# Two-bank score tiles, one exponential for two heads, a third column group as quads, and an earlier start of LayerNorm rows

## The chip, the cores and the metric

The kernel runs on one core of a Trainium2 chip. The metric is the device time of one execution in microseconds (us); less is better. TensorE (PE) does the matrix products, VectorE (DVE), ScalarE (ACT) and GpSimd (POOL) the rest, and SyncE (SP) issues most of the transfers.

## The reference

A transformer layer in fp32, with LayerNorm ahead of both halves, for 2048 tokens of width 640, 32 heads of 20, an inner width of 1536 and a causal window of 256.

```python
q, k, v = split(layernorm(x) @ wqkv)                 # 32 heads of 20
scores = q @ k.T * 20 ** -0.5                        # masked to 0 <= i - j < 256
h = x + (softmax(scores) @ v) @ wo
n = layernorm(h)
out = h + (gelu(n @ w_gate) * (n @ w_up)) @ w_down   # gelu by tanh
```

## The kernel before, in words

**Numbers.** Each fp32 factor is split into two f16 parts, a high and a low one (`xh`, `xl`, `w5h`, `w5l` and so on), and a product is the sum of three: high by high, high by low, low by high. All instructions go through one helper, so every row of the profile names line 199; they are told apart by the names of their tiles.

**Attention.** The 2048 tokens are 16 blocks of 128 queries, each with a window of up to three blocks of keys. The 32 heads are 16 pairs, the even head in the upper and the odd head in the lower half of PE's rows. Each row of work is done twice: `maxima` computes q by k into PSUM and `max_out` takes the greatest of each query on DVE (tile `junk`, with the result in `mxs`); `scores` computes k by q with the maxima subtracted through extra rows of `qT` and `kT`, and `score_out` takes the exponential on ACT into `pt`. POOL masks `pt`, and PE multiplies it by `v` into `pv`. Then come the product by `wo`, the row `h` (tile `ht`, stored by SP to `h_dram` for the end), and its LayerNorm.

**PSUM.** `bank(name)` hands out banks of rings: `mm` (2 banks), `ra` and `rb` (2 each), `pv` and `tp` (1 each). A row of maxima or scores takes both banks of `ra` or `rb`, one for each head; `two(name)` says when both are free. `row_need` chooses what the next row is. `ra` and `rb` also serve the early LayerNorm transposes and the scales of weights.

**Feed-forward.** Four chunks `c` of 512 tokens by three groups `fg` of 512 inner columns, in the order of the list `ORDER`: (0,0), (1,0), (0,1), (0,2), (1,1), (1,2), then chunks 2 and 3. The first `PLAIN` of these are done by `gate_up`: for each of four `ft` steps 30 matmuls of 512 columns into `mm`. The others are done by `quad`, which gets the same sums from nine spans of five matmuls (10 of 512 and 35 of 256 columns) into `tp`, `ra`, `pv` and `rb`, with the help of sums of weights (`weight_sums`, tile `ws`, made by POOL and DVE) and of tokens (`token_sums`, tile `ts`, made by DVE). Weight sums are stored to `wsums` and later loaded rather than made again, as `QLOAD` lists. `down` multiplies by `w_down` and adds into `ht`; between quads it fills PE. The names in the trace: `w5`/`w8` are gate and up of group 1, `w6`/`w9` of group 2, `gu` of group 0; `w10`, `w11`, `w12` are `w_down`; `h0h`/`h0l` and `h1h`/`h1l` are the normalised chunks.

**LayerNorm of h.** `first_norm_lane` normalises the four blocks of chunk 0 during the attention, from their tiles `ht` (`B[b].h`) into a tile `lxn`. `norm_start` starts two lanes of `norm_lane` for each later chunk: load a block's row from `h_dram` into a `wsl` tile, statistics (`lsth`, `lsti`), power by POOL, normalise, split, and turn it by DMA into the chunk's tiles, which for chunk 2 are those of chunk 0.

**Order.** No order is written out by hand. The kernel runs through lanes (generators) and a model of each engine's time (`Clock`); at each step it issues what the model says can start first. So a changed duration or a changed condition anywhere can change the order of everything after it. On the chip each engine runs its instructions in that recorded order. While no score has been issued and PE would stand idle in the model, a small matmul `pv<-ident16` is issued as filler.

Of the kernel before, what the change touches and what calls it, by code (L numbers as in the profile page):

```python
# [11 lines left out]
F32 = mybir.dt.float32  # L12
# [10 lines left out]
P = 128  # L23
# [230 lines left out]
def block_kernel(ctx: ExitStack, tc: tile.TileContext, x, wqkv, wo, wg, wu, wd, out):  # L254
# [9 lines left out]

    banks = dict(mm=2, ra=2, rb=2, pv=1, tp=1)

    opened, pos = Counter(), Counter()

    def bank(name, dt=F32):
        opened[name] += 1  # L270
        return nc.tile(psum, [P, 512 if dt == F32 else 1024], dt, name, banks[name])

# [29 lines left out]
    def need(*reads, slots=(), when=None, eng="tensor"):  # L302

        def f():
            if when and not when() or any(opened[n] >= banks[n] for n in slots):
                return INF
            return max([nc.ready(reads, eng)]
                       + [nc.slot(psum, n, banks[n]) for n in slots])
        return f
# [222 lines left out]
    def products(n, term, ready=None, at_=None):  # L532


        ps = [at_[0]] if at_ else []
        col = at_[1] if at_ else 0

        def start(i):
            if ready and not ready(i) or not ps and opened["mm"] >= banks["mm"]:
                return INF  # L540
            t = nc.ready([x for ab in term(i) for x in ab], "tensor")
            return t if ps else max(t, nc.slot(psum, "mm", banks["mm"]))

        for i in range(n):
            yield ("tensor",), lambda i=i: start(i)
            if not ps:
                ps.append(bank("mm"))
            m = term(i)
            for k, (l, r) in enumerate(m):
                if k:  # L550
                    yield pe()
                o = ps[0][:, col:col + r.free_size()]
                nc.tensor.matmul(o, l, r, start=(i == 0 and k == 0),
                                 stop=(i == n - 1 and k == len(m) - 1))
                pos["dense"] += r.free_size() * 3 // len(m)
        return o
# [17 lines left out]

    attn = ExitStack()
    wqp = ExitStack()
# [237 lines left out]
    def maxima(at_):  # L814
        j, pr = heapq.heappop(maxq)
        b = B[j]
        ps = [bank(at_) for _ in range(2)]
        n = len(window(j))
# [12 lines left out]
    def two(name):  # L831

        if opened[name]:
            return INF
        return max(nc.slot(psum, name, banks[name], k) for k in range(2))

# [89 lines left out]
    def scores(at_):  # L926
# [3 lines left out]
        if pr % 2 == 0:  # L930
            b.pt[u] = at("pt", [P, 4, 3, P], F32, 3)
            pos["units"] += 1
        n = len(window(j))
        ps = [bank(at_)[:, :pairs(j) * n * P].rearrange("p (k a b) -> p k a b", a=n, b=P)
              for _ in range(2)]
        for k in range(pairs(j)):
            for i, kb in enumerate(window(j)):
                for par in range(2):
                    rs = slice(64 * par, 64 * par + 62)
                    nc.tensor.matmul(ps[par][:, k, i, :], kT[rs, pr + k, kb % RK, :],  # L940
                                     b.c.qT[rs, pr + k, b.cols], start=True, stop=True)
        for par in range(2):
            tasks.append(score_out(j, pr, par, ps[par], b.pt[u], at_))
        pos["score"] += pairs(j)

    def score_out(j, pr, par, ps, pt, at_):
        b = B[j]
        u = pr // 2
        n = len(window(j))
        m = pairs(j)  # L950
        yield on("scalar", ps)
        if m > 1:
            nc.scalar.activation(pt[:, par::2, :n, :], ps, AF.Exp, scale=esc)
        else:
            nc.scalar.activation(pt[:, 2 * (pr % 2) + par, :n, :], ps[:, 0], AF.Exp, scale=esc)
        done(at_)
        pos[j, u] += m
        if pos[j, u] < 4:
# [103 lines left out]
    ORDER += [(c, fg) for c in range(2, NCH) for fg in range(FG)]  # L1062
    PLAIN = 4
    hts, ga = {}, {}
# [201 lines left out]
    def norm_start(c):  # L1266
        yield ("sync",), need(when=lambda: pos["gu", c - 2] == FG if c > 1 else (
            ffpools[0] and W["d", 0].ready and all(b.wrote for b in B[CB:2 * CB])), eng="sync")
# [8 lines left out]
    def norm_lane(c, bs, lane, t):  # L1277
        for b in bs:
            j = c * CB + b
            yield ("sync",), lambda: nc.others(t, "sync")  # L1280
            nc.sync.dma_start(t, h_dram[j * P:(j + 1) * P, :])
            yield from layernorm(t, lane, *hpart(c, b), xn=lambda: t, dma=True)
            chunk[c] += 1
# [5 lines left out]
    def token_sums(c):  # L1289
        hh, hl = hT[c]  # L1290
        h1, h2 = hh[:, :, :CW], hh[:, :, CW:]
        l1, l2 = hl[:, :, :CW], hl[:, :, CW:]
        yield on("vector", when=lambda: ffpools[1] and (c == 1 or W["d", FG - 1].ready))
        t = (nc.tile(ffp, [P, KC, 512], F32, "ts") if c % 2 else
             nc.tile(ffpools[0], [P, KC, 512], F32, "wst")).bitcast(F16)
# [14 lines left out]
    WS = {}  # L1310
    QLOAD = [(c, fg) for c in range(2, NCH) for fg in range(FG) if (c, fg) != (2, 0)]
    wsums = dram.tile([FG * FT, P, 4 * KC * P], F16, name="wsums")
# [92 lines left out]
    def dense_lane():  # L1405
# [238 lines left out]
```

## Time and profile before

| | |
|---|---|
| Time, median of 3 runs | 1042.01 us (1041.12 to 1042.12) |
| The profiled execution's own time | 1043.35 us |
| Its span | 1041.6 us |
| Granted TensorE clock, mean | 0.996 |
| PE, DVE, ACT, POOL busy | 98%, 75%, 47%, 26% |

The attention takes about the first 600 us of the span, the feed-forward the rest, with its first groups mixed into the last of the attention. In a row of instructions the first two numbers are start and duration in us, or start of a run of `xN` instructions; in brackets stand the idle time of the engine before it and what ended it. Matmuls are pipelined, so their cost is read from start to start. In a row of a group the numbers behind the bar are busy time in us and the mean duration of one in ns, behind the second bar the idle time before them and what ended it. In a row of windows each engine has its busy time and instruction count, then come the granted clock, the share of DMA and GB/s.

### The profile page before, as it was taken

The page shows a single profiled execution, that of the slowest core. Times are in us where ns is not written, and L with a number is a line of the kernel's source. Part 1 is how long each engine was busy: PE and PEld are TensorE (multiplying, and loading weights), DVE is VectorE, ACT ScalarE, POOL GpSimd, SP SyncE. Part 2 cuts the span into 40 slices and gives each one's busy share as a digit, 9 for nine tenths or more (in the row PEclk, how much of TensorE's full clock was granted, in tenths as well). Part 3 has the DMA queues.
Part 4 walks back from the last instruction along what each step waited for, and adds up shares of the span by engine and source line. Part 5 has one row for each costly group of instructions (what it writes and reads, how often), then busy time and mean ns, then how long its engine had stood idle before and what let it go on. Part 6 is the DMA issues. An engine that isn't in the chain of part 4 may idle for free.

```text
span 1041.6 us, 26895 instructions
## 1 busy us (share of the span) xinstructions
PE 1019.7 (98%) x10802; PEld 691.2 (66%) x10802; DVE 778.4 (75%) x2193; ACT 490.6 (47%) x938; POOL 269.8 (26%) x369
## 2 busy tenths in 40 slices
PE   8999999999999999999999899999999999999998
PEld 7876567667666666676655564555777777777776
DVE  6878989998787777677687867676997985445553
ACT  6512667666666766666667835341122222222220
POOL 7100332233333323232323511031445310000000
PEclk9999999999999999999999999999999999999999
DMA  8663354361341513415302341314342652122211
GB/s 300 149 133 114 119 121 132 122 150 55 73 107 43 101 45 77 77 44 112 129 28 90 78 139 52 101 51 127 102 144 110 164 166 77 59 94 102 77 51 51
DMA packets 89116, 105.86 MB, mean 102 GB/s; under 512 B 22176, under 2 KB 63392, under 8 KB 88992
## 3 DMA queue, kind: packets, MB, share of 16 engines
q1 hardware_dynamic: 76896, 93.41, 31.2%
q10 hardware_dynamic: 12096, 10.75, 3.2%
q8 instruction: 84, 1.38, 0.6%
q14 instruction: 40, 0.33, 0.1%
HBM read 71.11 MB, written 28.84 MB: 96 GB/s over the span
## 4 chain that ended last, share of the span: by engine, by line
PE 78%; DVE 13%; issue 3%; DMA 3%; ACT 2%; POOL 0%; SPq 0%; DVEq 0%; ACTq 0%
PE mm L199 40%; PE pv L199 11%; PE ra L199 11%; PE rb L199 9%; PE tp L199 7%; DVE junk L199 4%; DMA qT<-qk 1%; DVE am L199 1%; DMA wst<-in_wd_dram 1%; DVE m L199 1%; DVE al L199 0%; DVE ht L199 0%; ACT pt L199 0%; DVE qks L199 0%; DMA wsl<-h_dram 0%
## 5 line engine op out<-in xcount | busy, mean ns | idle before, releaser
L199 POOL TENSOR_SCALAR_AFFINE_SELECT pt<-pt 128x512 f32<-128x512 f32 x240 | 152.9, 659 | 361.4 <-ACT pt L199 358.7
L199 DVE CUSTOM_DVE_ANT_0 junk<-rb,mask 128x384 bf16<-128x384 f32 (+2 forms) x262 | 138.9, 530 | 42.4 <-PE rb L199 22.6
L199 DVE CUSTOM_DVE_ANT_0 junk<-ra,mask 128x384 bf16<-128x384 f32 (+2 forms) x250 | 132.2, 529 | 41.4 <-PE ra L199 22.3
L199 ACT ACTIVATE pt<-ra,esc 128x384 f32<-128x384 f32 (+2 forms) x248 | 130.7, 579 | 68.4 <-PE ra L199 57.3
L199 ACT ACTIVATE pt<-rb,esc 128x384 f32<-128x384 f32 (+2 forms) x232 | 122.0, 578 | 70.1 <-PE rb L199 59.2
L199 PE MATMUL pv<-pt,v 128*21 128x128 f32 x2880 | 104.8, 277 | 2.1 <-ACT oT L199 2.1
L199 PEld LDWEIGHTS <-ah 128*128 128x128 f16 x768 | 75.5, 98 | 31.1 <-issue 3.1
L199 ACT ACTIVATE gel<-gel,ffk 128x512 f32<-128x512 f32 x32 | 23.1, 722 | 121.4 <-DVE gel L199 121.4
L199 PEld LDWEIGHTS pv<-pt,v 128*21 128x21 f32 x2880 | 68.8, 101 | 17.0 <-ACT oT L199 2.8
L199 PEld LDWEIGHTS <-kT 62*128 62x128 f16 x1440 | 57.8, 95 | 22.7 <-issue 12.7
L199 PEld LDWEIGHTS <-ws 128*128 128x128 f16 x640 | 62.6, 98 | 7.2
L199 PEld LDWEIGHTS <-gu 128*128 128x128 f16 x440 | 42.1, 98 | 36.6 <-issue 1.5
L199 ACT CAST ah<-gel 128x512 f16<-128x512 f32 x48 | 29.6, 616 | 75.7 <-DVE gel L199 75.7
L199 DVE SCALAR_TENSOR_TENSOR ht<-mm,ffk,ht 128x320 f32<-128x320 f32 x96 | 51.9, 545 | 15.9 <-PE mm L199 13.8
L199 PEld LDWEIGHTS <-qT 60*128 60x128 f16 x640 | 24.5, 93 | 56.7 <-issue 55.3
L199 PE MATMUL mm<-xh,w1h 128*128 128x256 f16 x200 | 54.6, 273 | 1.6 <-DVE qks L199 1.6
L199 PE MATMUL mm<-xl,w1h 128*128 128x256 f16 x200 | 54.7, 273 | 0.0
L199 PE MATMUL mm<-xh,w1l 128*128 128x256 f16 x200 | 54.7, 273 | 0.0
L199 PE MATMUL mm<-w3h,oh 128*128 128x320 f16 x160 | 48.0, 300 | 0.1
L199 PE MATMUL mm<-w2h,xh 128*128 128x320 f16 x160 | 48.1, 300 | 0.0
L199 PE MATMUL mm<-w3l,oh 128*128 128x320 f16 x160 | 48.0, 300 | 0.0
L199 PE MATMUL mm<-w2h,xl 128*128 128x320 f16 x160 | 48.0, 300 | 0.0
(296 smaller groups left out, 2531.8 us busy)
## 6 DMA issues: line engine op xcount, KB each, us to landing
ws<-wsums SPq DMA_DIRECT2D x20, 640.0 KB
qk<-qks ACTq DMA_DIRECT2D x32, 256.0 KB
qT<-qk SPq DMA_DIRECT2D x48, 160.0 KB
kT<-qk SPq DMA_DIRECT2D x48, 160.0 KB
wsums<-ws SPq DMA_DIRECT2D x12, 640.0 KB
ht<-in_x_dram SPq DMA_DIRECT2D x16, 320.0 KB
h_dram<-ht SPq DMA_DIRECT2D x16, 320.0 KB
ht<-h_dram SPq DMA_DIRECT2D x16, 320.0 KB
```

Of the source, the lines that this page charges most:

```text
L199: r = real(*args, **kw)
```

## The change

Four edits in one.

1. During the attention, `ra` and `rb` are one tile of two banks each in a pool of their own, `psa`; each head uses one half. `score_out` is one task for both heads, with one exponential over both banks (768 columns for a full window; for the first two blocks of queries it is still two, now one for each pair). After the attention `ra` and `rb` are rings of two one-bank tiles again, in a new pool `psf`. What used one bank of `ra` or `rb` in the attention (the early transposes, the scales) now has one slot in place of two.
2. `PLAIN` is 3: (0,2) is done by quads too, so chunk 0 gets token sums (tile `ts0`). `QLOAD` is worked out from `ORDER`: weight sums of group 2 are made for (0,2), of group 1 for (1,1), of group 0 for (2,0), and loaded everywhere else. The lane of weight sums waits for the gate and up weights of its own group in place of the last `w_down`.
3. `norm_start` of chunks 2 and 3 asks for two finished column groups of the chunk two before it in place of three. Only the step that writes the shared tiles still waits for three.
4. `first_norm_lane` normalises in place, in `ht`, rather than into `lxn`. So that write has to wait for the store `h_dram<-ht`.

```diff
@@ -262,13 +262,19 @@
 
     h_dram = dram.tile([S, D], F32, name="h_dram")
 
-    banks = dict(mm=2, ra=2, rb=2, pv=1, tp=1)
+    banks = dict(mm=2, ra=1, rb=1, pv=1, tp=1)
 
     opened, pos = Counter(), Counter()
 
     def bank(name, dt=F32):
         opened[name] += 1
-        return nc.tile(psum, [P, 512 if dt == F32 else 1024], dt, name, banks[name])
+        n = (512 if dt == F32 else 1024) * (2 if name in wide else 1)
+        return nc.tile(psums[name], [P, n], dt, name, banks[name])
+
+    attn = ExitStack()
+    psa = attn.enter_context(tc.tile_pool(name="psa", bufs=1, space=PSUM))
+    psums = dict(mm=psum, pv=psum, tp=psum, ra=psa, rb=psa)
+    wide = {"ra", "rb"}
 
     def ps_tp(dt=F32):
         return bank("tp", dt)
@@ -814,7 +819,9 @@
     def maxima(at_):
         j, pr = heapq.heappop(maxq)
         b = B[j]
-        ps = [bank(at_) for _ in range(2)]
+        t = bank(at_)
+        ps = [t[:, 512 * par:512 * par + 512] for par in range(2)]
+        opened[at_] += 1
         n = len(window(j))
         for k in range(pairs(j)):
             for i, s, m in runs(j):
@@ -830,9 +837,7 @@
 
     def two(name):
 
-        if opened[name]:
-            return INF
-        return max(nc.slot(psum, name, banks[name], k) for k in range(2))
+        return INF if opened[name] else nc.slot(psums[name], name, banks[name])
 
     def row_need():
 
@@ -931,30 +936,29 @@
             b.pt[u] = at("pt", [P, 4, 3, P], F32, 3)
             pos["units"] += 1
         n = len(window(j))
-        ps = [bank(at_)[:, :pairs(j) * n * P].rearrange("p (k a b) -> p k a b", a=n, b=P)
-              for _ in range(2)]
+        t = bank(at_).rearrange("p (r c) -> p r c", r=2)[:, :, :pairs(j) * n * P]
+        ps = [t[:, par].rearrange("p (k a b) -> p k a b", a=n, b=P) for par in range(2)]
         for k in range(pairs(j)):
             for i, kb in enumerate(window(j)):
                 for par in range(2):
                     rs = slice(64 * par, 64 * par + 62)
                     nc.tensor.matmul(ps[par][:, k, i, :], kT[rs, pr + k, kb % RK, :],
                                      b.c.qT[rs, pr + k, b.cols], start=True, stop=True)
-        for par in range(2):
-            tasks.append(score_out(j, pr, par, ps[par], b.pt[u], at_))
+        tasks.append(score_out(j, pr, t, b.pt[u], at_))
         pos["score"] += pairs(j)
 
-    def score_out(j, pr, par, ps, pt, at_):
+    def score_out(j, pr, t, pt, at_):
         b = B[j]
         u = pr // 2
         n = len(window(j))
         m = pairs(j)
-        yield on("scalar", ps)
-        if m > 1:
-            nc.scalar.activation(pt[:, par::2, :n, :], ps, AF.Exp, scale=esc)
-        else:
-            nc.scalar.activation(pt[:, 2 * (pr % 2) + par, :n, :], ps[:, 0], AF.Exp, scale=esc)
+        yield on("scalar", t)
+        for k in range(m):
+            h = 2 * (pr % 2 + k)
+            nc.scalar.activation(pt[:, h:h + 2, :n, :].rearrange("p h a b -> p h (a b)"),
+                                 t[:, :, k * n * P:(k + 1) * n * P], AF.Exp, scale=esc)
         done(at_)
-        pos[j, u] += m
+        pos[j, u] += 2 * m
         if pos[j, u] < 4:
             return
         yield on("gpsimd", pt[:, :, 0, :])
@@ -1060,7 +1064,7 @@
     NCH = S // (CB * P)
     ORDER = [(0, 0), (1, 0), (0, 1), (0, 2), (1, 1), (1, 2)]
     ORDER += [(c, fg) for c in range(2, NCH) for fg in range(FG)]
-    PLAIN = 4
+    PLAIN = 3
     hts, ga = {}, {}
     ffpools = [None, None]
 
@@ -1264,7 +1268,7 @@
     lnbuf = []
 
     def norm_start(c):
-        yield ("sync",), need(when=lambda: pos["gu", c - 2] == FG if c > 1 else (
+        yield ("sync",), need(when=lambda: pos["gu", c - 2] == FG - 1 if c > 1 else (
             ffpools[0] and W["d", 0].ready and all(b.wrote for b in B[CB:2 * CB])), eng="sync")
         if c == 1:
             hT[1] = tuple(nc.tile(ffpools[0], [P, KC, CB * P], F16, n) for n in ("h1h", "h1l"))
@@ -1279,7 +1283,8 @@
             j = c * CB + b
             yield ("sync",), lambda: nc.others(t, "sync")
             nc.sync.dma_start(t, h_dram[j * P:(j + 1) * P, :])
-            yield from layernorm(t, lane, *hpart(c, b), xn=lambda: t, dma=True)
+            yield from layernorm(t, lane, *hpart(c, b), xn=lambda: t, dma=True,
+                                 when=lambda: c < 2 or pos["gu", c - 2] == FG)
             chunk[c] += 1
         if chunk[c] == CB:
             side.append((LATE, token_sums(c)))
@@ -1290,8 +1295,8 @@
         hh, hl = hT[c]
         h1, h2 = hh[:, :, :CW], hh[:, :, CW:]
         l1, l2 = hl[:, :, :CW], hl[:, :, CW:]
-        yield on("vector", when=lambda: ffpools[1] and (c == 1 or W["d", FG - 1].ready))
-        t = (nc.tile(ffp, [P, KC, 512], F32, "ts") if c % 2 else
+        yield on("vector", when=lambda: ffpools[1] and (c < 2 or W["d", FG - 1].ready))
+        t = (nc.tile(ffp, [P, KC, 512], F32, "ts" if c else "ts0") if c % 2 or not c else
              nc.tile(ffpools[0], [P, KC, 512], F32, "wst")).bitcast(F16)
         t = t.rearrange("p c (a n) -> p a c n", a=4)
         for ks in (slice(k, k + 1) for k in range(KC)):
@@ -1308,7 +1313,7 @@
         TS[c] = t
 
     WS = {}
-    QLOAD = [(c, fg) for c in range(2, NCH) for fg in range(FG) if (c, fg) != (2, 0)]
+    QLOAD = [q for i, q in enumerate(ORDER) if q[1] in [fg for _, fg in ORDER[PLAIN:i]]]
     wsums = dram.tile([FG * FT, P, 4 * KC * P], F16, name="wsums")
 
     def weight_sums(c, fg, ft):
@@ -1340,9 +1345,10 @@
         for b in range(CB):
             yield on("vector", when=lambda: B[b].halves == 2)
             yield from layernorm(B[b].h, "h", *hpart(0, b),
-                                 xn=lambda: nc.tile(lnp, [P, D], F32, "lxn"))
+                                 xn=lambda: B[b].h)
             B[b].normed = True
             chunk[0] += 1
+        side.append((LATE, token_sums(0)))
 
 
     later = [(kind, fg) for fg in range(FG) for kind in "gud"]
@@ -1446,6 +1452,10 @@
                     yield pe(when=lambda: woq or all(b.wrote for b in B))
         nonlocal ffp
         attn.close()
+        psf = ctx.enter_context(tc.tile_pool(name="psf", bufs=1, space=PSUM))
+        psums.update(ra=psf, rb=psf)
+        banks.update(ra=2, rb=2)
+        wide.clear()
         ffp = ctx.enter_context(tc.tile_pool(name="ffp", bufs=2, reuse_waits="tile"))
         ffpools[1] = ffp
         for c in range(1, NCH):
@@ -1470,7 +1480,8 @@
 
         def sums_lane():
             for i, q in enumerate(quads):
-                yield on("gpsimd", when=lambda: pos["quads"] >= i - 1 and W["d", 2].ready)
+                yield on("gpsimd", when=lambda: pos["quads"] >= i - 1 and W["g", q[1]].ready
+                         and W["u", q[1]].ready)
                 yield from weight_sums(*q)
 
         side.append((LATE, sums_lane()))
```

The other hunks only name the pool of a ring (`psums[...]`) where `psum` stood.

Counted over the whole order, PE's matmul instructions go from 9324 to 9405: 60 more for (0,2) (180 in place of 120) and 21 more fillers `pv<-ident16` (306 for 285). ACT's exponentials of 384 columns, 448, become 224 of 768. DVE has 40 more instructions.

First place: DVE where the second lot of column groups ends. `lsth<-wsl` is the statistics of the first row of chunk 2, `gel<-mm` the product that frees the up bank of an `ft` step, `am<-wst` the greatest of a weight tile. Before, at the end of (0,2):

```order
L199 TENSOR_TENSOR al<-gel,ah 128x512
L199 BN_STATS lsth<-wsl 128x6 x2
L199 BN_AGGR lmvh<-lsth 128x2
L199 TENSOR_SCALAR lveh<-lmvh 128x1
L199 SCALAR_TENSOR_TENSOR lyah<-lyh,lveh 128x1
L199 TENSOR_SCALAR lyah<-lyah 128x1
L199 TENSOR_TENSOR lyh<-lyh,lyah 128x1
L199 TENSOR_SCALAR wsl<-wsl,lmvh,lyh 128x640
L199 BN_STATS lsti<-wsl 128x6
L199 SCALAR_TENSOR_TENSOR gel<-mm,ffk,gel 128x512
```

And in the change, at the end of (0,1):

```order
L199 TENSOR_TENSOR al<-gel,ah 128x512
L199 TENSOR_REDUCE am_11105<-wst 128x1 x5
L199 TENSOR_REDUCE am_11105<-am_11105 128x1
L199 TENSOR_SCALAR am_11105<-am_11105 128x1
L199 BN_STATS lsth<-wsl 128x6 x2
L199 SCALAR_TENSOR_TENSOR gel<-mm,ffk,gel 128x512
L199 TENSOR_REDUCE am_11105<-tp 128x1
L199 BN_AGGR lmvh<-lsth 128x2
```

The statistics that stood ahead of the last `gel<-mm` of (0,2) stand ahead of the last `gel<-mm` of (0,1), behind the maxima of the last weight tile.

Second place: PE where (0,2) begins, behind the last matmuls of `down` for (1,0) (`w10`). Before:

```order
L199 LDWEIGHTS al
L199 MATMUL mm<-w10h,al 128x320
L199 LDWEIGHTS w6h
L199 MATMUL mm<-h0h,w6h 128x512
L199 LDWEIGHTS w6h
L199 MATMUL mm<-h0l,w6h 128x512
```

And in the change:

```order
L199 LDWEIGHTS al
L199 MATMUL mm<-w10h,al 128x320
L199 LDWEIGHTS w6l
L199 MATMUL tp<-h0h,w6l 128x256
...
L199 LDWEIGHTS ws
L199 MATMUL tp<-ts_10661,ws 128x256
```

The second span of the first quad needs weight sums right here, behind five matmuls; before, they were first needed after the whole of (0,2) and of `down` for (0,1).

Third place: SP around the second store of a finished row `ht` in the attention; each piece begins at or just ahead of the first store. Before:

```order
L199 DMA kT<-qk_1367 20x16x256 x2
L199 DMA h_dram<-ht 128x640
L199 DMA kT<-qk_1367 20x16x256 x4
L199 DMA xt<-in_x_dram 128x640
L199 DMA h_dram<-ht 128x640
```

And in the change:

```order
L199 DMA h_dram<-ht 128x640
L199 DMA qT<-qk_1284 20x16x256
L199 DMA kT<-qk_1437 20x16x256 x6
L199 DMA wsl<-in_wg_dram 128x512 x2
L199 DMA wsl<-in_wu_dram 128x512
L199 DMA xt<-in_x_dram 128x640
L199 DMA wsl<-in_wu_dram 128x512 x2
L199 DMA h_dram<-ht 128x640
```

Loads of weights and of x, each of which waits for a free buffer, now stand between the first and the second store.

More of the change, by code (lines that the diff above doesn't have):

```diff
@@ L307, in f @@
             return max([nc.ready(reads, eng)]
-                       + [nc.slot(psum, n, banks[n]) for n in slots])
+                       + [nc.slot(psums[n], n, banks[n]) for n in slots])
         return f
@@ L541, in start @@
             t = nc.ready([x for ab in term(i) for x in ab], "tensor")
-            return t if ps else max(t, nc.slot(psum, "mm", banks["mm"]))
+            return t if ps else max(t, nc.slot(psums["mm"], "mm", banks["mm"]))
         for i in range(n):
@@ L572, in ff_scales_down @@
                                 _pow2(-GE - XE - UE - GE - WE), op0=ALU.mult, op1=ALU.mult)
-    attn = ExitStack()
     wqp = ExitStack()
```

## The prediction

> **What bounds the kernel now.** I read the page's busy times and chain first.
>
> ```profile
> span 1041.6 us, 26895 instructions
> PE 1019.7 (98%) x10802; PEld 691.2 (66%) x10802; DVE 778.4 (75%) x2193; ACT 490.6 (47%) x938; POOL 269.8 (26%) x369
> PE 78%; DVE 13%; issue 3%; DMA 3%; ACT 2%; POOL 0%; SPq 0%; DVEq 0%; ACTq 0%
> ```
>
> PE is busy for 98% of the span and carries 78% of the chain that ended last; ACT, on which the largest edit acts, is busy for 47% and is 2% of the chain. So a microsecond counts only where PE issues fewer columns or waits less. Then I read the busy time by stretches of 25 us: the attention's early part, the two stretches around the change from plain groups to quads, and the first full stretch of quads.
>
> ```profile
> 100.00:125.00 25.00, 23.21 (x247) 13.06 (x246) 23.28 (x77) 17.32 (x37) 8.21 (x12) 0.96 0.43 134
> 625.00:650.00 25.00, 24.84 (x117) 11.22 (x116) 18.06 (x40) 13.75 (x21) 5.19 (x4) 1.00 0.15 53
> 700.00:725.00 25.00, 23.00 (x123) 12.61 (x122) 17.22 (x34) 4.68 (x7) 5.83 (x5) 0.93 0.34 108
> 725.00:750.00 25.00, 25.00 (x187) 18.11 (x185) 22.42 (x47) 4.59 (x7) 7.48 (x7) 1.00 0.35 91
> ```
>
> Columns are PE, PEld, DVE, ACT and POOL busy, then the granted clock. At 100 to 125 us DVE is at 23.28 of 25 and PE loses 1.8: there DVE sets the pace. At 700 to 725 us PE loses 2.0 and the clock falls to 0.93. From 725 us PE is full. The profiled run took 1043.35 us, 1.75 more than its span, and lies 1.34 above the median of 1042.01. I work the change out against this run and take the difference from the median. A measurement of this kernel can tell about 0.2%, 2.1 us, from no change.
>
> **Part 1: chunk 0's third column group as quads (PLAIN 4 to 3).** A plain `ft` step is 30 matmuls of 512 columns; a quad is 45 matmuls, 10 of 512 and 35 of 256. The first two rows give the pace of the plain ones (7 steps apart), the others the start of a quad and of what follows it.
>
> ```profile
> 710.78 0.38 PE L199 MATMUL mm<-h0l,w9h 128*128 128x512 f16 x1
> 712.29 0.38 PE L199 MATMUL mm<-h0h,w9l 128*128 128x512 f16 x1
> 729.38 0.71 PE L199 MATMUL tp<-h1h,w5l 128*128 128x256 f16 x5
> 735.35 0.30 PE L199 MATMUL mm<-w12h,ah 128*128 128x320 f16 x1
> ```
>
> (712.29 − 710.78) / 7 = 0.216 us, so the four plain steps take 120 × 0.216 = 25.9 us. A quad takes 735.35 − 729.38 = 5.97, four take 23.9. Gain: **−2.0 us**. Beside it come 20 DVE operations of token sums for chunk 0 (at most 0.42 us each by the median of their kind, 7 us in all) among the plain groups of 600 to 675 us, where DVE has 25 − 18.06 = 6.9 idle in one stretch of 25 alone: nothing, and some 1 us if they crowd a waiting operation. SP issues four more loads of weight sums (24 for 20), off the chain.
>
> ```profile
> L199 DVE SCALAR_TENSOR_TENSOR ts<-ts,h1l x10: 412/420/833, 616.7 to 858.2; 128x256 f16<-128x256 f16 x10
> ```
>
> **Part 2: the LayerNorm of chunk 2 starts a column group sooner.** This is where 700 to 725 us loses its time. PE, DVE and SP there:
>
> ```profile
> 714.00 0.30 PE L199 MATMUL mm<-w11h,al 128*128 128x320 f16 x1
> 716.29 0.30 PE L199 MATMUL mm<-w11h,ah 128*128 128x320 f16 x1 [2.00 <-DVE gel L199]
> 711.95 0.89 DVE L199 BATCH_NORM_STATS2 lsth<-wsl 128x6 f32<-128x320 f32 x2 [3.52 <-DMA wsl<-h_dram]
> 715.50 0.73 DVE L199 SCALAR_TENSOR_TENSOR gel<-mm,ffk,gel 128x512 f32<-128x512 f32 x1
> 702.68 5.02 SPq L199 DMA_DIRECT2D wsums<-ws x2
> 707.74 1.38 SPq L199 DMA_DIRECT2D wsl<-h_dram x2
> 716.00:721.00 5.00, 4.71 (x23) 2.87 (x23) 3.53 (x10) 0.62 (x1) 0.55 (x1) 0.66 0.54 127
> ```
>
> SP issues the row load only at 707.74, behind a store of weight sums. DVE stands in order at the statistics of that row for 3.52 us; behind them waits the last `gel<-mm`, and behind that PE's next `mm` bank. PE's step is 716.29 − 714.00 = 2.29 us in place of 0.14 (the pace of these matmuls), a loss of 2.15. Right after, the granted clock is 0.66 over 5 us: 0.34 × 5 = 1.7 us more. One group sooner this load goes out before any store of weight sums. The old place is rid of 2.15 + 1.7 = **−3.85 us**.
>
> The Trainium skill (TensorE: Matmul & The Clock Gate, "What's actually happening") says that the array drops to half clock after at least one idle window of some 3.4 us. By that rule the hole of 2.15 us would not have cost the clock, which would then fall for a reason of its own. The trace's 0.66 right behind a hole shorter than such a window speaks against it.
>
> The 1.7 stays in the sum, and its return is a rival below.
>
> The wait does not vanish: the statistics now stand ahead of the last `gel<-mm` of (0,1). Before, there:
>
> ```profile
> 665.57 2.23 SPq L199 DMA_DIRECT2D wst<-in_wu_dram x5
> 670.55 2.13 DVE L199 TENSOR_REDUCE am<-wst 128x1 f32<-128x512 f32 x3 [0.98 <-DMA wst<-in_wu_dram]
> 672.59 0.74 DVE L199 SCALAR_TENSOR_TENSOR gel<-mm,ffk,gel 128x512 f32<-128x512 f32 x1
> 672.17 0.30 PE L199 MATMUL mm<-w10h,ah 128*128 128x320 f16 x1
> ```
>
> PE starts the first group of `down` at 672.17 and wants the second bank 12 × 0.136 = 1.6 later, at 673.8; `gel<-mm` ends at 673.3, 0.5 ahead. Now 0.89 of statistics come first, which alone is a stall of 0.4. The row load is issued behind the five weight loads, at about 667.8; with the 4.2 us that it took from 707.74 to 711.95 it would land at 672.0, in time, but those five weight loads land until about 672, so it may be 1 us late. Bounds: 0.4, and 3 if the 1 us of lateness is there and the clock falls too (1.4 + 1.7). I take **+1.0**, near the lower end, which the 4.2 us give.
>
> The same delay moves the weights of the first quad. In the trace of before the last low part `w9l` is done at 682.3, and weight sums take POOL 1.84 and DVE two operations of 0.81 each:
>
> ```profile
> 680.88 1.40 DVE L199 SCALAR_TENSOR_TENSOR w9l<-wst,sw,w9h 128x512 f16<-128x512 f32 x2
> 696.38 1.84 POOL L199 TENSOR_TENSOR ws<-w5l,w8l 128x640 f16<-128x640 f16 x1
> 699.63 0.81 DVE L199 SCALAR_TENSOR_TENSOR ws<-w8h,w8l 128x640 f16<-128x640 f16 x1
> ```
>
> On DVE the statistics and gel push the scale of `w9` back by some 2.2 us (0.89 of statistics, about as much for the second row's, the rest wait and small operations), so `w9l` is done at 684.5 and the sums that the quad's second span reads about 3.5 later, at 688. PE gets there at 672.17 + 96 × 0.136 + 1.0 + 0.55 = 686.8. Stall: **+1.1**, between 0 (POOL and DVE begin early) and 3 (they queue behind the LayerNorm).
>
> **Part 3: two-bank tiles and one exponential for two heads.** 448 Exps of 384 become 224 of 768 (those of 128 and 256 columns keep their number).
>
> ```profile
> 300.86 0.58 ACT L199 CAST xh<-tp 128x512 f16<-128x512 f32 x1 [0.68 <-PE tp L199]
> 301.54 1.05 ACT L199 ACTIVATE pt<-ra,esc 128x384 f32<-128x384 f32 x2
> 306.02 0.58 ACT L199 ACTIVATE pt<-ra,esc 128x384 f32<-128x384 f32 x1 [1.42 <-POOL pt L199]
> 306.50 0.26 ACT L199 CAST xh<-tp 128x128 f16<-128x128 f32 x1
> L199 PE MATMUL ra<-qT,kT 62*128 62x128 f16 x744 | 43.6, 216 | 1.1 <-DVE mxs L199 0.6 <-ACT pt L199 0.3
> L199 PE MATMUL rb<-kT,qT 60*128 60x384 f16 x166 | 29.7, 332 | 1.8 <-DVE mxs L199 1.0 <-ACT pt L199 0.5
> ```
>
> Two Exps of 384 take 1.05. A copy of 512 takes 0.58 and one of 128 takes 0.26, 0.83 ns an element, so one of 768 should take 0.58 + 384 × 0.83 ns = 0.90. That saves 0.15 × 224 = 34 us of ACT, which has time to spare; it counts only where PE waits for `pt`. Those waits are 0.3 + 0.5 in the two rows and as much again in the rows for the other combinations and inside groups: **−1.0** (0 to −2). What the two-bank tile takes away, that one head's bank is free before the other's, was worth little, since the planner opened both banks of a ring together and the matmuls alternate between the heads.
>
> With other durations the planner writes another order for the whole attention. By the stalls of the stretch at 100 us (1.8) and its likes I give this 0 ± 3. At the start, while the ring that the early LayerNorm transposes use has one slot, PE gets 21 more filler matmuls (306 for 285):
>
> ```profile
> 10.60 1.06 PE L199 MATMUL pv<-ident 128*128 128x128 f16 x16
> ```
>
> 21 × 1.06 / 16 = **+1.4 us**, if fillers stand for time that PE has to pass there anyway.
>
> **Part 4: LayerNorm of chunk 0 in place.** Now `ht<-ht` must wait until the store `h_dram<-ht` has read the row. The last of the four blocks before:
>
> ```profile
> 236.96 0.33 SPq L199 DMA_DIRECT2D h_dram<-ht x1
> 245.00 0.61 DVE L199 TENSOR_SCALAR lxn<-ht,lmvh,lyh 128x640 f32<-128x640 f32 x1
> ```
>
> The store is issued 8 us before the normalised row is written; taking the load's 4.2 us for the store too, 4 us remain. Those 4 us of statistics and small operations on a crowded DVE are the cover: **0**. If SP reaches the store that much later, DVE stands, with the maxima behind it and PE behind them.
>
> **Sum.** −2.0 − 3.85 + 1.0 + 1.1 − 1.0 + 1.4 + 0 = −3.35, against the profiled run 1040.0, against the median 1042.0 − 3.35 = **1038.7 us**.
>
> **Rivals.**
> - *The hole only moves* (the change does not do what it says): the row load lands 3 us late behind the weight loads, and the hole at 674 us costs what the old one did, 3.85 in place of 1.0. Sum −0.5: 1041.5. For it: DVE was waiting 0.98 for those weight loads already. Against: no store of weight sums is ahead on SP.
> - *The clock falls anyway.* The 0.66 after 716 us does not hang on the hole but on the mix of work there, and comes back at the same place or behind one of the two stalls of 1 us: 1.7 of the gain is lost, sum −1.65, 1040.4. For it: the hole is short. Against: no other place of the feed-forward after 650 us shows it (the stretch from 725 us has 1.00).
> - *Slower: DVE waits for the store.* In part 4 SP is held by a load of x or of weights that waits for its buffer, and the store goes out late for the four blocks between 145 and 245 us, where DVE has 1.7 of 25 us to spare. Beyond the cover each us goes to PE. At 3 us a block it is +12, so +8.7: 1050.7. It decides against the forecast from 3.35 / 4 = 0.8 us a block. For it: in the new order loads of weights and x stand ahead of the second store. Against: 4 us of cover.
> - *Better: the attention's order relaxes.* With 34 us less on ACT, the planner's new order takes 3 us out of the stalls of the early attention: 1035.7. For it: 1.8 us are lost in one stretch of 25 there. Against: DVE is what is full there, and its work is the same.
>
> **Chances.** Forecast (1036.5 to 1041) 0.42; hole moves 0.16; clock falls anyway 0.07; DVE waits for the store, or the new order costs as much in the same stretch, 0.22; better 0.13. Faster by over 0.2% (below 1039.9): the better case's 0.13, 0.39 of the forecast's (all but its upper end) and 0.03 of the clock's, 0.55. Within 0.2%: 0.16, 0.03 and 0.04, 0.23. Slower: 0.22. The range, 1034 to 1047, takes in the better case, the moved hole and the cheaper half of the slower one.
>
> **What would show it.** Right: no DVE wait on `wsl<-h_dram` above 710 us and a granted clock of 1.00 there; four quads on `h0` of about 6 us each from 686 us; a stall of about 1 us before the second `down` group of (1,0) and one before the first `tp<-ts,ws`; Exps of 128x768 at 0.90. Wrong: a granted clock below 1.00 at 672 to 690 us (the hole moved); DVE `ht<-ht` with idle time before it put down to a DMA; PE's loss between 100 and 225 us more than 3 us above before's; and, if all of that is in order, an end of the attention that has moved by more than 3 us.

## The result and the profile after

The changed kernel took 1034.98 us (median of 6 runs, 1033.42 to 1037.35) beside 1042.12 for the kernel before (6 runs, 1041.12 to 1044.94): 7.1 us less, ratio 0.9925, 95% interval 0.9914 to 0.9937. Run again, beside other kernels, it gave 1032.52 beside 1043.3, ratio 0.990 (0.9884 to 0.9915). Forecast were 1038.7 and a range of 1034 to 1047: the first measurement lies 1.0 us above its lower end, the second 1.5 below it. The ratios are not those of the two medians, so the two ways of telling a gain differ by up to 1.4 us (by its ratio the first measurement is a gain of 7.8). Below, a gain over the kernel before goes by the ratio, and a difference between two changed kernels by their medians.

The page of the changed kernel: span, busy times and the chain.

```profile
span 1035.2 us, 26653 instructions
PE 1012.8 (98%) x10883; PEld 696.4 (67%) x10883; DVE 789.2 (76%) x2233; ACT 460.8 (45%) x718; POOL 272.2 (26%) x373
PE 81%; DVE 10%; DMA 3%; issue 2%; ACT 2%; ACTq 0%; SPq 0%; POOL 0%; DVEq 0%; POOLq 0%
```

The last of these lines would suggest that little has changed but DVE's share of the chain (13% before). ACT has 30 us less to do, where 34 had been worked out (with the first edit alone it is 32.4). The exponentials on the page, and one pair's worth in the timeline of the second run of the changed kernel:

```profile
L199 ACT ACTIVATE pt<-rb,esc 128x768 f32<-128x768 f32 (+2 forms) x131 | 110.9, 855 | 80.9 <-PE rb L199 75.1
```

```profile
180.22 0.90 ACT L199 ACTIVATE pt<-rb,esc 128x768 f32<-128x768 f32 x1
181.02 0.58 ACT L199 COPY oT<-pv 128x512 f32<-128x512 f32 x1
```

One of 768 takes 0.90 us, the value worked out. The stretches before, from attention to end (before first, then after; the cut lies where `gate_up` of (0,1) ends on PE):

```profile
100.00:600.00 500.00, 488.73 (x6875) 319.82 (x6873) 405.44 (x1322) 337.61 (x681) 163.88 (x258) 1.00 0.35 91
672.00:1042.00 370.00, 364.08 (x2622) 257.03 (x2620) 247.71 (x486) 81.44 (x126) 73.48 (x68) 0.99 0.30 97
```

```profile
100.00:600.00 500.00, 491.06 (x6939) 322.36 (x6937) 410.09 (x1333) 305.44 (x456) 163.74 (x258) 0.99 0.34 90
669.00:1036.00 367.00, 360.77 (x2683) 261.81 (x2681) 251.33 (x506) 83.90 (x130) 75.63 (x72) 1.00 0.32 103
```

In the attention PE gets more of its matmuls into the same 500 us (6939 for 6875), and `gate_up` of (0,1) ends at 669.4 us where it ended at 672.2. From there to PE's last matmul it was 366.1 us and is 362.5: 3.6 of the span's 6.4 us come from the feed-forward, where 3.75 (−2.0 − 3.85 + 2.1) had been forecast, and 2.8 from ahead of it, where a loss of 0.4 had been. Half clock hides the true shares: by the clock records of the traces, before lost 1.7 us to it at 123 us and 1.7 at 717 us, the changed kernel 1.7 at 100 us and 1.7 at 145 us. Without these the feed-forward gives 1.9 us and what is ahead of it 4.5. The stalls of PE and what DVE does at the new place, in the timeline of the changed kernel:

```profile
669.93 0.49 PE L199 MATMUL tp<-ident,am 128*128 128x128 f32 x2 [0.39 <-DVE am L199]
679.67 0.30 PE L199 MATMUL mm<-w10h,ah 128*128 128x320 f16 x1 [1.00 <-DVE ht L199]
683.74 0.30 PE L199 MATMUL mm<-w10h,ah 128*128 128x320 f16 x1 [0.50 <-DVE ht L199]
```

```profile
669.80 0.88 DVE L199 BATCH_NORM_STATS2 lsth<-wsl 128x6 f32<-128x320 f32 x2
670.59 0.73 DVE L199 SCALAR_TENSOR_TENSOR gel<-mm,ffk,gel 128x512 f32<-128x512 f32 x1
677.88 0.61 DVE L199 TENSOR_SCALAR wsl<-wsl,lmvi,lyi 128x640 f32<-128x640 f32 x1
678.40 0.75 DVE L199 SCALAR_TENSOR_TENSOR w9l<-wst,sw,w9h 128x512 f16<-128x512 f32 x1
679.07 0.55 DVE L199 SCALAR_TENSOR_TENSOR ht<-mm,ffk,ht 128x320 f32<-128x320 f32 x1
```

No wait stands at the statistics: the row had landed, and the last `gel<-mm` is in time. The first stall is for the maxima `am` of a weight tile, whose loads DVE had waited for. Later the `ht<-mm` of a `down` group stands behind LayerNorm and weight operations on DVE, and PE waits for its bank.

### The profile page after: what moved, and what is told of

Read it like the earlier page. It is cut to its first block, busy times and chain, and to the rows that moved or that the text cites. A ratio compares the mean times of both kernels' runs of the same rounds, so it can differ in the third digit from the quotient of the medians.

```text
span 1035.2 us, 26653 instructions
## 1 busy us (share of the span) xinstructions
PE 1012.8 (98%) x10883; PEld 696.4 (67%) x10883; DVE 789.2 (76%) x2233; ACT 460.8 (45%) x718; POOL 272.2 (26%) x373
## 4 chain that ended last, share of the span: by engine, by line
PE 81%; DVE 10%; DMA 3%; issue 2%; ACT 2%; ACTq 0%; SPq 0%; POOL 0%; DVEq 0%; POOLq 0%
PE mm L199 39%; PE pv L199 13%; PE ra L199 12%; PE rb L199 10%; PE tp L199 8%; DVE junk L199 4%; DVE am L199 1%; DMA qT<-mT 1%; DMA kT<-qk 1%; DVE m L199 1%; DMA wsl<-in_wo_dram 1%; DVE ht L199 1%; DMA qk<-qks 0%; DMA wst<-in_wg_dram 0%; DMA wst<-in_wu_dram 0%
## 5 line engine op out<-in xcount | busy, mean ns | idle before, releaser
L199 DVE CUSTOM_DVE_ANT_0 junk<-ra,mask 128x384 bf16<-128x384 f32 (+2 forms) x258 | 136.9, 530 | 36.4 <-PE ra L199 30.4
L199 DVE CUSTOM_DVE_ANT_0 junk<-rb,mask 128x384 bf16<-128x384 f32 (+2 forms) x254 | 134.8, 531 | 35.7 <-PE rb L199 28.1
L199 ACT ACTIVATE pt<-rb,esc 128x768 f32<-128x768 f32 (+2 forms) x131 | 110.9, 855 | 80.9 <-PE rb L199 75.1
L199 ACT ACTIVATE pt<-ra,esc 128x768 f32<-128x768 f32 (+2 forms) x125 | 107.7, 867 | 72.9 <-PE ra L199 68.9
L199 ACT ACTIVATE gel<-gel,ffk 128x512 f32<-128x512 f32 x36 | 26.0, 721 | 138.5 <-DVE gel L199 134.4
L199 PEld LDWEIGHTS <-ws 128*128 128x128 f16 x720 | 70.3, 98 | 8.3
L199 PE MATMUL mm<-xh,w0h 128*128 128x256 f16 x175 | 48.3, 276 | 0.0
L199 PE MATMUL mm<-xh,w0l 128*128 128x256 f16 x175 | 48.2, 275 | 0.0
L199 PE MATMUL mm<-xl,w0h 128*128 128x256 f16 x175 | 48.2, 275 | 0.0
```

The costliest lines, as they stand in the source:

```text
L199: r = real(*args, **kw)
```

## The experiments

They were run in three groups; the kernels of a group shared one chip and the runs of the kernel before on it.

**First group: the edits one by one.** The first edit alone (two-bank tiles, one exponential for two heads), the second with the fourth, the third, and the fourth, each put on the kernel before:

```diff
+    psums = dict(mm=psum, pv=psum, tp=psum, ra=psa, rb=psa)
+    wide = {"ra", "rb"}
...
+            nc.scalar.activation(pt[:, h:h + 2, :n, :].rearrange("p h a b -> p h (a b)"),
+                                 t[:, :, k * n * P:(k + 1) * n * P], AF.Exp, scale=esc)
```

> Before with the first edit alone: two-bank tiles and one exponential for two heads. Theory A (the part of the gain that the prediction missed, some 3 us ahead of 670 us, is this edit's: PE no longer stops in the middle of a score or maxima row for the second head's bank): 3 us faster than before, 1039, and steps of over 100 ns inside score rows fall from 17 to a few. Theory B (the missed part is the luck of another order): within 1.5 us of before, although those steps fall away too.

Measured: 1034.92, ratio 0.9935 (0.9923 to 0.9948): 6.8 us faster. Steps of over 100 ns from start to start between neighbouring matmuls of a score row fell from 18 to 2. So this edit alone gives about the whole of the first measurement (their intervals overlap), more than either theory expected.

```diff
-    PLAIN = 4
+    PLAIN = 3
...
+        side.append((LATE, token_sums(0)))
...
-                                 xn=lambda: nc.tile(lnp, [P, D], F32, "lxn"))
+                                 xn=lambda: B[b].h)
```

> Before with the second and the fourth edit (quads for (0,2), LayerNorm of chunk 0 in place; the second doesn't fit in memory without the fourth). Columns alone give -2.0 us. The wait for the row load stays behind the stores of weight sums. If that hole falls on quads, which don't use the mm banks that the last gel<-mm frees, it costs PE little and the run is 2 to 5 us faster than before; if it still stops a down group, 2 us faster and no more.

Measured: 1039.18, ratio 0.997 (0.9958 to 0.9981): 3.1 us faster. PE shows no stall above 0.5 us behind 690 us in this trace, although the third edit is not in it: the statistics of chunk 2's first row come at 725 us, among quads, and nothing waits for them.

```diff
-        yield ("sync",), need(when=lambda: pos["gu", c - 2] == FG if c > 1 else (
+        yield ("sync",), need(when=lambda: pos["gu", c - 2] == FG - 1 if c > 1 else (
```

> Before with the third edit alone. Theory A (the hole of 2.15 us with 1.7 us of half clock at 714 to 720 us is gone, one of about 1 us comes at 672 to 685 us): 2.8 us faster than before, 1039.3, clock 1.00 from 700 to 725 us. Theory B (the hole moves with its clock): within 1 us of before.

Measured: 1041.58, ratio 0.9989 (0.9976 to 1.0002): 1.1 us faster, with no change inside the interval and theory A's 2.8 outside it. The hole at 714 us is gone in its trace and the clock is 1.00 from 700 to 725 us; a new hole stands at 684 us:

```profile
684.09 0.30 PE L199 MATMUL mm<-w10h,ah 128*128 128x320 f16 x1 [1.09 <-DVE ht L199]
```

The fourth edit alone has the diff's last line above.

> Before with the fourth edit alone. Theory A (4 us of cover hide the store): within 1 us of before, and no idle time of DVE ahead of ht<-ht that a DMA ended. Rival: DVE stands there, some us per block for four blocks, and the run is over 2 us slower.

Measured: 1043.22, ratio 1.0002 (0.9989 to 1.0016): no change. The group of in-place rows in this kernel's trace has no idle time before it:

```profile
L199 DVE TENSOR_SCALAR ht<-ht,lmvh,lyh 128x640 f32<-128x640 f32 x4 | 2.4, 603 | 0.0
```

PE's hole of 714 us is there too. Its row in this kernel's timeline, and the windows around it:

```profile
717.84 0.30 PE L199 MATMUL mm<-w11h,ah 128*128 128x320 f16 x1 [1.81 <-DVE gel L199]
```

```profile
715.00:720.00 5.00, 3.19 (x24) 2.16 (x23) 4.41 (x11) 1.34 (x2) 0.45 (x1) 1.00 0.17 33
720.00:725.00 5.00, 5.00 (x39) 3.62 (x37) 3.98 (x12) 0.72 (x1) 0.55 (x1) 1.00 0.43 104
```

It is 1.81 us here and the granted clock stays at 1.00: the 1.7 us of half clock behind the hole in the first profile are not a fixed part of it.

**Second group: what in the first edit counts.** The changed kernel once more:

> The changed kernel once more, on the same chip as the three runs beside it: about 7 us faster than before, and level with the first edit alone (6.8 us), since the other edits gave 3.1 and about 1 when made alone. Its half clock between 100 and 150 us (3.4 us in the first profile) belongs to one execution, if it is 1.7 or nothing here.

Measured: 1032.52, ratio 0.990 (0.9884 to 0.9915), 10.4 us faster: more than the first edit alone gave (6.8), by about what the second and fourth gave (3.1), so the expected level with the first edit alone did not come. Its profiled execution, span 1028.8 and the fastest of its five, has a granted clock of 1.00 from 100 to 150 us, where the first profile of the same kernel lost 3.4.

Then the same kernel with each exponential split, and nothing else on any engine changed, order included:

```diff
-            nc.scalar.activation(pt[:, h:h + 2, :n, :].rearrange("p h a b -> p h (a b)"),
-                                 t[:, :, k * n * P:(k + 1) * n * P], AF.Exp, scale=esc)
+            o = pt[:, h:h + 2, :n, :].rearrange("p h a b -> p h (a b)")
+            i = t[:, :, k * n * P:(k + 1) * n * P]
+            for par in range(2):
+                nc.scalar.real.activation(o[:, par], i[:, par], AF.Exp, scale=esc)
+            nc.issue("scalar", nc.scalar.cost("activation", o, [i, esc]), [i, esc], [o])
```

> The changed kernel with each Exp of 768 made as two of 384 behind each other, every other instruction and the order as in the changed kernel. Theory A (the shorter exponential is what edit 1 gives): 34 us more on ACT, 3 to 5 us slower than the changed kernel. Theory B (the ring of two-bank tiles and the order it brings give it): within 1 us of the changed kernel, since ACT is at 45%.

Measured: 1039.14, ratio 0.9956 (0.9943 to 0.997): 6.6 us slower than the changed kernel beside it (5.8 by the ratios); the intervals are apart. PE, DVE and POOL run the same instructions in the same order in both traces. PE, DVE and ACT of the two pages, the changed kernel first:

```profile
PE 1008.5 (98%) x10883; PEld 694.6 (68%) x10883; DVE 787.6 (77%) x2233; ACT 461.1 (45%) x718; POOL 273.3 (27%) x373
```

```profile
PE 1013.2 (98%) x10883; PEld 697.0 (67%) x10883; DVE 789.8 (76%) x2233; ACT 497.7 (48%) x974; POOL 274.0 (26%) x373
```

ACT goes from 45% to 48%, by 36.6 us, and the kernel loses 6.6 of it. In the profiled executions the spans differ by 7.7, and 3.4 of that is half clock in the split one's attention, so some 4.3 us are stalls. The groups of the maximum and value matmuls that differ most, the changed kernel first:

```profile
L199 PE MATMUL pv<-pt,v 128*21 128x128 f32 x2880 | 104.0, 275 | 2.4 <-ACT oT L199 2.4
L199 PE MATMUL rb<-kT,qT 60*128 60x384 f16 x156 | 26.2, 332 | 0.0
```

```profile
L199 PE MATMUL pv<-pt,v 128*21 128x128 f32 x2880 | 104.0, 275 | 3.6 <-ACT oT L199 3.4 <-POOL pt L199 0.2
L199 PE MATMUL rb<-kT,qT 60*128 60x384 f16 x156 | 26.5, 334 | 1.8 <-ACT pt L961 1.4 <-DVE mxs L199 0.3
```

PE waits 1.0 us more for the copy `oT<-pv`, which stands behind an exponential on ACT, and 1.4 more for a bank that an exponential still reads. All waits of PE that ACT ended come to 5.4 us in the split trace, 2.4 in the changed kernel's, and 2.2 to 3.0 in the five others that have the first edit and nothing added to ACT (3.4 before, in another order). The rest is in steps too small for these lists, and in half clock, some of which seems to follow from these waits. One place shows how. With the two exponentials the copy ends later, as these rows of the split trace show beside the two of the changed kernel above:

```profile
184.03 1.05 ACT L961 ACTIVATE pt<-rb,esc 128x384 f32<-128x384 f32 x2
184.98 0.59 ACT L199 COPY oT<-pv 128x512 f32<-128x512 f32 x1
```

and PE waits 0.15 us longer for it, the changed kernel first:

```profile
181.65 0.62 PE L199 MATMUL pv<-pt,v 128*21 128x128 f32 x14 [1.53 <-ACT oT L199]
185.61 0.64 PE L199 MATMUL pv<-pt,v 128*21 128x128 f32 x16 [1.68 <-ACT oT L199]
```

Behind the hole of 1.68 the clock falls to half for 3.41 us, from 186.77 on. The hole is 1.53 in all six traces that have the first edit and nothing added to ACT, and no half clock follows it in any of them.

The changed kernel without the first edit:

```diff
-    banks = dict(mm=2, ra=1, rb=1, pv=1, tp=1)
+    banks = dict(mm=2, ra=2, rb=2, pv=1, tp=1)
...
+        for par in range(2):
+            tasks.append(score_out(j, pr, par, ps[par], b.pt[u], at_))
```

> The changed kernel without the first edit: rings of one-bank tiles and an exponential for each head. If the edits add up, it is 4 us faster than before (3.1 + 1.1), 3 to 4 slower than the changed kernel; if edits 2 and 3 share one gain (both take the hole at 714 us away), 3 faster than before and 4 to 5 slower than the changed kernel.

Measured: 1040.88, ratio 0.9977 (0.9964 to 0.999): 2.4 us faster than before and 8.4 slower than the changed kernel, where at most 5 had been expected. With the third edit in it, it is no better than the second and fourth alone (3.1).

LayerNorm of chunk 2 still sooner:

```diff
-pos["gu", c - 2] == FG - 1 if c > 1 else (
+pos["gu", c - 2] == FG - 1 if c > 2 else pos["gu", 1] >= 1 if c > 1 else (
```

> The changed kernel with the LayerNorm rows of chunk 2 started one more column group sooner, when (1,0) is done, so that its statistics stand among the plain steps of (0,1) and not among the down groups of (1,0). Theory A (the 2.4 us of stalls at 670 to 684 us come from those statistics in DVE's queue): 1.5 to 2.4 us faster than the changed kernel. Rival (DVE has as much to do there anyway, and a plain step waits instead): within 1 us of it.

Measured: 1034.14, ratio 0.991 (0.9896 to 0.9924), within noise of the changed kernel (0.990). In its trace the stretch from the end of (0,1) to PE's last matmul is 361.0 us where the changed kernel's two profiles have 362.5 and 362.5, so the stalls moved by it are worth 1.5 us; that is less than the two runs' intervals can tell apart.

**Third group.** ACT loaded without making any exponential longer:

```diff
                                  t[:, :, k * n * P:(k + 1) * n * P], AF.Exp, scale=esc)
+            nc.scalar.real.activation(dose, ident[:, :96], AF.Copy)
```

> The changed kernel with a small ACT operation of 96 columns behind each exponential, which reads a constant and writes a scratch tile that nothing reads; all else and the order as in the changed kernel. It takes about as much of ACT's time as the split did (some 0.15 us each, 38 us in all), but the exponential before it ends as early as in the changed kernel. Theory A1 (what counts is how soon one row's exponential ends and lets its bank go): within 1.5 us of the changed kernel. Theory A2 (what counts is the load on ACT's queue, whatever stands in it): 4 to 7 us slower than the changed kernel, like the split.

Measured: 1037.62, ratio 0.9943 (0.9928 to 0.9959). In the same group the changed kernel without its third edit, which below turns out level with the changed kernel, took 1032.85 (ratio 0.9905, 0.9888 to 0.9922): 4.8 us less, the intervals apart. The load behind it is 41 us by the page:

```profile
PE 1012.2 (98%) x10883; PEld 697.3 (67%) x10883; DVE 790.1 (76%) x2233; ACT 502.2 (49%) x974; POOL 273.3 (26%) x373
```

The scratch operations release nothing that PE waits for. They can only delay what stands behind them on ACT: copies, casts and the next exponentials, whose banks then come free later. This trace has both, 5.6 us of waits that ACT ended in all. The largest, with total, times and longest:

```profile
PE pv L199 <- ACT oT L199: 3.6, 4, 1.7
PE rb L199 <- ACT pt L199: 1.0, 1, 1.0
PE ra L199 <- ACT pt L199: 0.7, 1, 0.7
```

The hole behind the copy at 183 us is 1.70 here, and a half clock follows it as in the split run. So the load on ACT's queue, whatever stands in it, brings the same waits as the split (5.4 us): theory A2. The price is less sure than the 4.8: beside the two measurements of the changed kernel itself, 0.990 and 0.9925, this run's ratio of 0.9943 is a loss of 4.5 and of 1.9 us, the second with intervals that overlap. Whether the split costs more than this load can't be told.

The changed kernel without the third edit:

```diff
-pos["gu", c - 2] == FG - 1 if c > 1 else (
+pos["gu", c - 2] == FG if c > 1 else (
...
-            yield from layernorm(t, lane, *hpart(c, b), xn=lambda: t, dma=True,
-                                 when=lambda: c < 2 or pos["gu", c - 2] == FG)
+            yield from layernorm(t, lane, *hpart(c, b), xn=lambda: t, dma=True)
```

> The changed kernel without the third edit: the LayerNorm rows of chunk 2 start when (0,2) is done, now among quads. If the third edit still gives what it gave alone (1.1 us), this is 1 us slower than the changed kernel. If the quads make that hole harmless (they don't need the bank that the last gel<-mm frees) and the third edit only brings the 2.4 us of stalls at 670 to 684 us, this is 1 to 2.5 us faster than the changed kernel.

Measured: 1032.85, ratio 0.9905 (0.9888 to 0.9922), level with the changed kernel, where it was to be 1 to 2.5 us faster or 1 slower. It has no hole at 714 us either, and its stretch from the end of (0,1) on is 361.0 us, 1.5 less than with the third edit (361.2 in the trace of the second and fourth edit alone).

(0,1) by quads too:

```diff
-    PLAIN = 3
+    PLAIN = 2
```

> The changed kernel with PLAIN = 2: (0,1) by quads too. Columns alone give another 2.0 us. If DVE and POOL can make the weight sums of group 1 beside the plain steps of (1,0), 2 us faster than the changed kernel; if PE waits for them at the first quads of (0,1), level or slower.

Measured: 1046.23, ratio 1.0037 (1.0022 to 1.0053), 3.9 us slower than before. PE waits at the first quads of (0,2) for their weight sums, in this kernel's timeline:

```profile
691.75 1.25 PE L199 MATMUL tp<-ts,ws 128*128 128x256 f16 x5 [8.53 <-DVE ws L199]
```

So `PLAIN` = 3 is where the saving of columns ends: one group sooner, the sums are late. The clock is at half from 685.4 to 695.6 us here, in the hole and behind it.

## Why the prediction was right, and where it was not

**The direction and the range were right**, but the forecast gain, 3.35, is half of the one measured, and it was made of the wrong parts. That the range held is in part luck: its lower end stood for "the attention's order relaxes", which had a chance of 0.13, the first measurement lies outside the 1036.5 to 1041 of the forecast itself, and the second lies below the range. The feed-forward, without its half clock, came out near the forecast (1.9 us for 2.05); the miss is in the attention.

**Quads for (0,2): right.** −2.0 was forecast from columns; the first of the four quads takes what one of (1,1) took (5.98 us from `tp<-h0h,w6l` at 685.37 to the next `mm<-w11` at 691.35 in the trace after). Alone, with the in-place LayerNorm that makes room for it, this edit gave 3.1 (2.0 to 4.4).

**The hole at 714 us: the place was right, the size and the remedy were not.** The step "the old place is rid of 2.15 + 1.7" counted in full a half clock that such a hole brings in some executions only: the same hole, 1.81 us long, had the full clock in the fourth edit alone, and with the third edit alone the gain was 1.1 (−0.2 to 2.5), not 2.8. The rival "the clock falls anyway" is out: of the other traces only the one with `PLAIN` = 2 has a half clock between 600 us and PE's last matmul. And the third edit is not what takes the hole away here: (0,2) as quads does so by itself (second and fourth edit alone; changed kernel without the third), because what waits for the bank that `gel<-mm` frees is then gone. With quads in place the third edit moves nothing but DVE's work in between the `down` groups of (1,0), at a cost of 1.5 us by the traces, which the runs can't tell from nothing.

**The new stalls: right in sum (2.1 forecast, 0.55 + 1.17 + 0.67 = 2.4 us by PE's late steps) by luck, wrong in their causes.** The row had landed and `gel` was not late; the stalls are one for `am` of the weights and two for `ht<-mm` behind LayerNorm and weight operations on DVE, and no quad waited for weight sums.

**One exponential for two heads: its own duration right (0.90), its worth wrong by a factor of some four to seven.** The step that failed is "it counts only where PE waits for `pt`": 0.8 us in two rows and as much again elsewhere, 1.6, of which −1.0 was taken. Split and nothing else, the exponentials cost 6.6 us. The waits that a list puts down to `pt` are only a part: ACT also holds the copies `oT<-pv` that PE's next matmuls need, in the same queue, behind the exponentials. Of the 3.0 us that the split adds to the waits ended by ACT, 1.8 are for `pt` and 1.2 for `oT`; the run with idle load adds much the same, 1.7 and 1.5. Longer waits may also bring a half clock, as one followed the hole at 184 us in both. Together this is most of the 6.6, not all of it; the rest is not shown wait by wait. ACT's 47% busy is a mean; what counts is how long an operation that PE is about to need stands behind others in ACT's queue.

**Tiles, order and fillers: 0 ± 3 and +1.4 forecast.** Between the split run (two-bank tiles, two exponentials) and the run without the first edit lie 2.2 us in favour of the tiles and their order (1.7 by the medians; ratios 0.9956 and 0.9977, intervals overlapping). The fillers cost nothing that shows: the first row of maxima starts at 51.87 us, where it started at 54.09 (51.5 to 52.1 in the traces with the first edit, 53.1 to 54.1 in those without), and the first score row at 92.33 for 99.12, in the split run at 91.98. How much of this is the tiles and how much the order was not tried. The steps inside score rows, which the two-bank tiles do away with, are not the main part: the split run has 5 of them, where before has 18 and the changed kernel 3 and 1 in its two profiles.

**In place: right.** No wait, no change. In the changed kernel too the four in-place rows have no idle time before them. The rival "DVE waits for the store" is out. "The hole only moves" had the wrong cause (the row load was in time), but the new stalls of 2.4 us are no smaller than the 2.15 of the old hole. "The attention's order relaxes" came true in its place (2.8 us ahead of 670 us in the first profile) but through shorter waits on ACT itself more than through another order: the split run has the new order and still lost 6.6 us.

## What to carry to other kernels

An engine at half load can still set the time of the one at 98%: price a shorter operation by what stands behind it in its in-order queue and who needs that next, and test it by splitting the operation back without touching the order, or by loading the queue with work that nobody reads. Before counting a half clock into a hole's price, look whether another execution has it, and count it as a chance. When two edits remove the same wait, count the gain once, and ask what the second one still costs.

## What the runs showed of the hardware

By the clock records of the traces the granted clock is full or half, and a half lasts 3.41 us or two or three times that (6.83, 10.24). Where PE is busy, 3.41 us of it lose 1.7. It comes in some executions and not in others of the same kernel: twice between 100 and 150 us in the first profile of the changed kernel, never there in the second (mean clock 0.997 and 1.0). The runs of one kernel in one group spread by 2 to 8 us (1030.48 to 1035.62 for the changed one, the width of three such halves).

The halves follow holes in PE's work, and where a hole falls counts. Within a trace they begin on a grid of 3.41 us, counted from the trace's first change of the clock. Here are two windows of that grid with the one behind each, from before and from the first profile of the changed kernel:

```profile
713.42:716.83 3.41, 1.41 (x11) 0.87 (x9) 2.79 (x7) 1.28 (x2) 0.48 (x1) 1.00 0.00 0
716.83:720.24 3.41, 3.41 (x15) 1.95 (x13) 2.32 (x7) 0.06 (x1) 0.35 (x1) 0.50 0.61 119
```

```profile
141.28:144.69 3.41, 1.21 (x13) 0.91 (x14) 1.95 (x7) 0.56 (x1) 0.00 (x0) 1.00 0.50 157
144.69:148.10 3.41, 3.41 (x22) 2.21 (x21) 1.96 (x7) 1.83 (x3) 0.66 (x2) 0.50 0.62 128
```

PE was idle for 2.0 and 2.2 us of one window, and the next was at half. Over all thirteen traces, between 60 us and PE's last matmul, 14 windows that began at the full clock have PE idle for 1.69 us or more, about half of them, and a half clock follows 12; of the shorter ones it follows five, all near 120 us. The two exceptions had 1.81 and 1.78 us, so there is no sharp threshold in idle time alone. The hole of 2.15 us was followed by a half clock, and holes of 1.81 and 1.25 us at the same place in other kernels were not. By the Trainium skill (TensorE: Matmul & The Clock Gate, "What's actually happening") the window is free-running and takes a whole idle one of 3.4 us to drop the clock. The first half of the rule fits the grid and the spread; the second does not: no half clock in these traces begins behind a window that was idle throughout, the most idle one being 2.80 us.
